# The last 64 rows of w1 by eight small transfers, a result sum in two PSUM tiles, and twice as many block-turned key groups in four batches

## Chip, core, metric

One core of a Trainium2 chip. The metric is the device time of one execution in microseconds, the median of several runs; comparisons are made with runs of the kernel before on the same chip.

## What is computed

One decode step of a gated mix: `g * a + (1 - g) * b` for 8 sequences of one token, 448 channels, in bf16.

```python
g = sigmoid((A_x * gate_w).sum(-1, keepdims=True))            # one gate per sequence
# a: attention over the last W = 1024 of 4096 cached positions, 16 query heads on 8 key heads, Dh = 256
q = (A_x @ A_wq).reshape(8, 1, 16, 256)
p = softmax(q . k[:, :, 3072:4096] * 256 ** -0.5)
a = (p . v[:, :, 3072:4096]).reshape(8, 1, 4096) @ A_wo       # 4096 x 448
# b: an MLP on the normalized A_x
y = layernorm(A_x)
b = gelu(y @ B_w1 + B_b1) @ B_w2 + B_b2                        # w1 448 x 1792, w2 1792 x 448
```

The keys and values that are read make 8 x 8 x 1024 x 256 x 2 tensors x 2 bytes, 67 MB of the 78 MB that the kernel reads.

## The kernel before

**The stream.** All large inputs go through a ring of four slots of 32 KB a partition (tile `slot`), in the order of a list: the keys of batch 0, wq, then keys of batch b and values of batch b - 1 in turn, then w1, the values of batch 7 with w2 behind them, and wo. A batch's keys or values are 4 MB, two transfers of 2 MB issued by SP (L128); weights are issued by SP at L140 and L157. `done()` frees a slot once its user's instructions are written down, and `pump()` then records the next load; on the chip SP waits at that load until the slot's readers have ended and until one of eight completion semaphores, used in turn by all loads, is free. SP works in order, so a load that waits holds up those behind it. x and the gate row are loaded by ACT, and so are the two biases (`biases`, L184), recorded in the transposing of batch 1's keys.

w1 has 448 rows. The first 384 lie on 128 partitions, three rows each (`w1_m`). The last 64 (`w1_t`) are cut in halves, so that one transfer of 128 rows of 896 elements fills all 128 partitions: even partitions hold a row's first half, odd ones its second. The same is done with the last 64 rows of wq.

**The batches.** For each batch b the kernel, in one fixed order per engine (nothing is reordered by a scheduler), does:

- `transpose_keys(b)`: sixteen groups of 4 x 128 columns (f32 words, two bf16 each) are turned so that the head dimension lies on the partitions. Group 0 is turned in 32 x 32 blocks by DVE into the tile `B` (`turn_blocks`, L330), and POOL puts the blocks in place in 16 copies (L338). Groups 1 to 15 go through PE (four transposes to a PSUM tile `ktp`, L360), and ten of them are copied to `kt` by ACT (L366), the other five by DVE (L368). Between the groups, at places given by `steps(b - 1)`, stand the softmax of the batch before (exponentials on ACT, `EB`, `EZ`, `ET` on DVE, one matmul `sm`) and the sums of the batch before that.
- `scores(b)`: 32 matmuls from `kt` (L427), which need all groups, POOL's too; `top(b)`, the row maximum on DVE (L440).
- `values(b - 1)`: 32 matmuls on the value slot into `PO` (L498).

**The MLP.** `norm` normalizes x, and `turned(1, ...)` lays it out as stationary operands `xw`; the shuffles of both biases follow in it (L307 to L310), recorded in the transposing of batch 2. `mlp_hidden` comes after the last batch's softmax: twelve matmuls for the first 384 rows (L538), and two for the last 64 (L549). Each of the two takes a stationary operand of 72 or 104 columns, zero in all but the wanted ones, so that one matmul serves two output blocks and even and odd partitions pick their halves.

**The end.** `hs` and the attention result `oP` are multiplied with w2 and wo: 40 wide matmuls into `A1` (L632), of 448 columns; `accs` is `A1` plus the bias (L639). The last six chunks of wo and the sum of `accs` over its four blocks go narrowly, 112 columns at a time, to four places of one PSUM tile, `A2` (L643). wo comes in seven pieces; the last four matmul chunks hang on the last two. `A2` is then copied to `res`, two blocks by DVE and two by ACT (L656), and each half is stored, by SP and by ACT (L657).

Of the kernel before, what the change touches and what calls it, by code (L numbers as in the profile page):

```python
# [11 lines left out]
BF16 = mybir.dt.bfloat16  # L12
F32 = mybir.dt.float32
# [4 lines left out]
def kernel(  # L18
# [15 lines left out]
    nc = tc.nc  # L34
# [19 lines left out]
    FQ = F // QD  # L54
    FB = FQ // BL
    HH = HD // 2
    FH = F // 2
    QN = 512
    NG = Hkv // QD
    SK = P // QD  # L60
    NCK = W // SK
    CB = 4
    UR = NG * rep
    HALF = D // 2
    DO = D // QD
# [79 lines left out]
    wq_m = A_wq[0:DM, :].rearrange("(p r) n -> p (r n)", r=NR)  # L145
    wq_t = A_wq[DM:D, :].rearrange("r (h n) -> (r h) n", h=2)
    w1_m = B_w1[0:DM, :].rearrange("(p r) f -> p (r f)", r=NR)
    w1_t = B_w1[DM:D, :].rearrange("r (h n) -> (r h) n", h=2)
    w2_v = B_w2.rearrange("(p c) n -> p (c n)", c=FB)
    wo_v = A_wo.rearrange("(q p j) n -> p q (j n)", p=P, j=J8)  # L150
    OW1T = NR * F
    OW2 = OW1T + FH
    wq_r = [wq_m[:, r * HD : (r + 1) * HD] for r in range(NR)]

    def last_values(t):
        kv_loader(A_v_cache, NB - 1, (2, 2), True)(t)
# [3 lines left out]
    add(("wq",), rows_loader(wq_r + [wq_t]))  # L160
    for b in range(1, NB):
        add(("k", b), kv_loader(A_k_cache, b))
        add(("v", b - 1), kv_loader(A_v_cache, b - 1))
    add(("w12",), rows_loader([w1_m, w1_t]))
    add(("v", NB - 1), last_values)
    cuts = [(q, 0, J8) for q in range(NQW - 2)] + [
        (NQW - 2, 0, 4),
# [14 lines left out]
    nc.scalar.dma_start(g_r[0:1, :], gate_w.rearrange("(o d) -> o d", o=1))  # L182

    def biases():  # L184
        nc.scalar.dma_start(b2_r[0:1, :], B_b2.rearrange("(o d) -> o d", o=1))
        nc.scalar.dma_start(b1_r[::BL, :], B_b1.rearrange("(t d) -> t d", t=QD))

    ident = consts.tile([P, P], BF16)
    make_identity(nc, ident[:])
# [23 lines left out]
    def turned(a, src):  # L213
        dst = xs[a][0:NB]
        nc.vector.tensor_copy(
            dst[:, 0:NR, :], src[:, 0:DM].rearrange("b (p r) -> b r p", r=NR)
        )
        for h in range(2):
            nc.vector.tensor_copy(dst[:, NR + h, h::2], src[:, DM:D])
        xt = work.tile([BL, NX, QD, BL], BF16, tag=f"w{2 + a}", name="xt")  # L220
        nc.vector.transpose(
            xt[:].rearrange("p r i b -> p (r i b)"),
            xs[a][:].rearrange("p r d -> p (r d)"),
        )
        for i in range(QD):
            nc.vector.tensor_copy(
                xw[BL * i : BL * (i + 1), a, :, BL : BL + NB], xt[:, :, i, 0:NB]
            )
# [66 lines left out]
    def norm():  # L295
        nc.vector.reciprocal(rstd[:], rstd[:])
        y_sb = consts.tile([NB, D], BF16)
        nc.vector.tensor_scalar(
            y_sb[:],
            x_sb[:],  # L300
            scalar1=mv[:, 0:1],
            scalar2=rstd[:],
            op0=ALU.subtract,
            op1=ALU.mult,
        )
        turned(1, y_sb[:])
        nc.vector.stream_shuffle(b1_b[:], b1_r[:], [0] * BL)  # L307
        b2_b = work.tile([BL, D], BF16, tag="w1", name="b2_b")
        nc.vector.stream_shuffle(b2_b[:], b2_r[:], [0] * BL)
        nc.vector.tensor_scalar_mul(b2s[0:NB, :], b2_b[0:NB, :], om[:])  # L310
# [4 lines left out]
        o = (a * NX + r) * GAP + BL  # L315
        return flat[:, o : o + NB]

    def ends(a, x2):
        o = (a * NX + NR) * GAP
        m = GAP + NB + BL * x2  # L320
        o += 0 if x2 else BL
        return flat[:, o : o + m], m
# [2 lines left out]

    BY_ACT = (1, 3, 4, 6, 7, 8, 10, 11, 13, 15)

    def turn_blocks(kn, kt, c0):
        B = epool.tile([P, CB, QD, SK // QD, QD], F32, tag="B", name="B")
        nc.vector.transpose(  # L330
            B[:].rearrange("p c w s a -> p (c w s a)"),
            kn[:, c0 * P : (c0 + CB) * P],
        )
        S8 = SK // QD
        words = kt[:].bitcast(F32)
        for w in range(QD):
            for g in range(QD):
                nc.gpsimd.tensor_copy(  # L338
                    words[BL * w : BL * (w + 1), :, c0 : c0 + CB, g * S8 : (g + 1) * S8, 0],
                    B[BL * g : BL * (g + 1), :, w].rearrange("p c s a -> p a c s"),  # L340
                )

    def transpose_keys(b, between=None):
        between = between or {}
        kn = slot("k", b)[:].bitcast(F32)
        for hh in range(NG):
            kt = ktpool.tile([P, QD, NCK, SK, NJ], BF16, tag="kt", name="kt")
            KT[hh] = kt
            for i in range(NCK // CB):
                g = hh * (NCK // CB) + i  # L350
                if g == 0:
                    turn_blocks(kn, kt, 0)
                    for step in between.get(g, ()):
                        step()
                    continue
                ktp = ps_kt.tile([P, CB, P, NJ], BF16, tag="ktp", name="ktp")
                words = ktp[:].bitcast(F32)
                for c in range(CB):
                    o = (hh * NCK + i * CB + c) * P
                    nc.tensor.transpose(  # L360
                        words[:, c, :, 0], kn[:, o : o + P], ident_f[:]
                    )
                dst = kt[:, :, i * CB : (i + 1) * CB, :, :]
                src = ktp[:].rearrange("p c (s a) t -> p a c s t", a=QD)
                if g in BY_ACT:
                    nc.scalar.copy(dst, src)  # L366
                else:
                    nc.vector.tensor_copy(dst, src)  # L368
                for step in between.get(g, ()):
                    step()  # L370
        done()

    def query():
        w = slot("wq")
        for r in range(NR):
            for n in range(W // QN):
                for t in range(QD):
                    o = r * HD + t * W + n * QN
                    nc.tensor.matmul(
                        S_ps[BL * t : BL * t + NB, n * QN : (n + 1) * QN],  # L380
                        lhsT=stationary(0, r),
                        rhs=w[:, o : o + QN],
                        start=(r == 0),
                        stop=False,
                        skip_group_check=True,
                    )
        for n in range(W // QN):
            for x2 in range(2):
                lhsT, m = ends(0, x2)
# [12 lines left out]
        qt = work.tile([P, 2, rep, QD, NJ, BL], BF16, tag="w2", name="qt")  # L402
        for h in range(2):
            nc.vector.transpose(  # L404
                qt[:, h].rearrange("p r i j b -> p (r i) j b"),
                qs[:, h * W // 2 : (h + 1) * W // 2].rearrange(
                    "p (m e j) -> p m j e", e=BL, j=NJ
                ),
            )
        qv = qw[:].rearrange("p j b t (u m) -> p j b t u m", u=NG)  # L410
        for i in range(QD):
            for g in range(QD):
                dst = qv[
                    BL * i : BL * (i + 1), :, :, 2 * (g % 2) : 2 * (g % 2) + 2, g // 2, 0:rep
                ]
# [115 lines left out]
    def mlp_hidden():  # L531
# [3 lines left out]
        for r in range(NR):  # L535
            for t in range(QD):
# [6 lines left out]
                    stop=False,  # L543
                    skip_group_check=True,
                )
        for x2 in range(2):
            lhsT, m = ends(1, x2)
            o = OW1T + x2 * FQ
            nc.tensor.matmul(  # L549
                hp[0:m, :],  # L550
                lhsT=lhsT,
                rhs=w[:, o : o + FQ],
                start=False,
                stop=(x2 == 1),
                skip_group_check=True,
            )
        z = work.tile([P, FQ], F32, tag="w0", name="z")
# [22 lines left out]
    def steps(b):  # L580
# [12 lines left out]
            d[15] = [biases]  # L593
        if b == 1:
            d[14] = [norm]
        return d

    transpose_keys(0, {7: [moments]})
# [20 lines left out]
    finish(b)  # L619
    spread(b)  # L620

    A2 = ps_kt.tile([P, DO], F32, tag="ktp", name="A2")
    w2 = slot("w12")
    w = slot("wo")
    NCH = NQW * J8
# [15 lines left out]
    for i, (lhsT, rhs) in enumerate(narrow):  # L641
        for t in range(QD):
            nc.tensor.matmul(  # L643
                A2[BL * t : BL * t + NB, :],
                lhsT=lhsT,
                rhs=rhs[:, t * DO : (t + 1) * DO],
                start=(i == 0),
                stop=(i == TAIL),
            )
    for h, (eng, copy) in enumerate(  # L650
# [2 lines left out]
        res = consts.tile([NB, 2, DO], BF16, name=f"res{h}")  # L653
        for i in range(2):
            t = 2 * h + i
            copy(res[:, i, :], A2[BL * t : BL * t + NB, :])  # L656
        eng.dma_start(  # L657
            out_f[:, h * HALF : (h + 1) * HALF], res[:].rearrange("b i d -> b (i d)")
        )
# [30 lines left out]
```

## Time and profile before

| | us |
|---|---|
| runs, median (three: 193.46 to 194.31) | 194.25 |
| profiled execution, its own time | 193.19 |
| its span, from first to last instruction | 191.4 |
| DMA queue q1, busy share of 16 engines | 96.3% |
| PE / DVE / ACT / POOL busy | 119.1 / 108.7 / 91.9 / 55.4 |
| mean rate of the DMA engines | 407 GB/s |
| granted clock of TensorE, mean | 0.854 |

The page describes the profiled execution. Its slices cut the span into 40 equal parts of 4.8 us; a digit is a busy share in tenths. "Idle before" of a group is the time its engine stood before it, with what ended it. Issue-to-landing times of DMAs include their wait in the queue. The trace also has a record for every DMA packet: queue, size, start and duration. q8 and q14 fetch instructions, q1 carries SP's transfers and q10 ACT's. All times in the text count from the first instruction, unless said otherwise.

### The profile page before, as it was taken

The page shows a single profiled execution, that of the slowest core. Times are in us where ns is not written, and L with a number is a line of the kernel's source. Part 1 is how long each engine was busy: PE and PEld are TensorE (multiplying, and loading weights), DVE is VectorE, ACT ScalarE, POOL GpSimd, SP SyncE. Part 2 cuts the span into 40 slices and gives each one's busy share as a digit, 9 for nine tenths or more (in the row PEclk, how much of TensorE's full clock was granted, in tenths as well). Part 3 has the DMA queues.
Part 4 walks back from the last instruction along what each step waited for, and adds up shares of the span by engine and source line. Part 5 has one row for each costly group of instructions (what it writes and reads, how often), then busy time and mean ns, then how long its engine had stood idle before and what let it go on. Part 6 is the DMA issues. An engine that isn't in the chain of part 4 may idle for free.

```text
span 191.4 us, 2916 instructions
## 1 busy us (share of the span) xinstructions
PE 119.1 (62%) x1114; PEld 77.0 (40%) x1114; DVE 108.7 (57%) x248; ACT 91.9 (48%) x105; POOL 55.4 (29%) x143
## 2 busy tenths in 40 slices
PE   0658509679784397738773676669854885083552
PEld 0646104555671185317641563168514761010111
DVE  4284673964889467705870687037822885847311
ACT  2298420894992259525852594228822892000001
POOL 8480000570750066005700480049002910000000
PEclk9999855999999969996999999756997999855555
DMA  5999999999999999999999999999999999999980
GB/s 204 445 402 425 440 435 419 425 421 432 422 430 428 428 421 431 426 431 428 418 431 425 421 435 428 428 428 416 431 431 428 425 425 420 403 422 430 407 321 3
DMA packets 7129, 77.86 MB, mean 407 GB/s; under 512 B 830, under 2 KB 1228, under 8 KB 1996
## 3 DMA queue, kind: packets, MB, share of 16 engines
q1 hardware_dynamic: 7072, 77.67, 96.3%
q8 instruction: 8, 0.13, 0.3%
q14 instruction: 5, 0.04, 0.1%
q10 hardware_dynamic: 44, 0.02, 0.0%
HBM read 77.67 MB, written 0.01 MB: 406 GB/s over the span
## 4 chain that ended last, share of the span: by engine, by line
DMA 73%; PE 10%; DVE 7%; ACT 4%; SPq 2%; issue 2%; DVEq 0%; ACTq 0%
DMA slot<-in_A_k_cache_dram 42%; DMA slot<-in_A_v_cache_dram 14%; DMA slot<-in_A_wq_dram 9%; DMA slot<-in_A_wo_dram 8%; PE ktp L360 7%; ACT kt L366 3%; DVE kt L368 2%; PE S_ps L427 2%; DVE qw L419 1%; SPq L128 1%; SPq L140 1%; DVE EZ L462 1%; PE S_ps L391 1%; DVE qt L404 1%; DVE nmx L440 1%
## 5 line engine op out<-in xcount | busy, mean ns | idle before, releaser
L366 ACT COPY kt<-ktp 128x1024 bf16<-128x1024 bf16 x80 | 76.1, 1024 | 37.0 <-PE ktp L360 36.9
L360 PE MATMUL ktp<-ident_f,slot 128*128 128x128 f32 x480 | 71.7, 305 | 31.4 <-DMA slot<-in_A_k_cache_dram 22.9
L360 PEld LDWEIGHTS ktp<-ident_f,slot 128*128 128x128 f32 x480 | 60.2, 157 | 49.2 <-issue 23.6
L338 POOL COPY kt<-B 32x128 f32<-32x128 f32 x128 | 51.3, 401 | 97.8 <-DVE B L330 86.3
L368 DVE COPY kt<-ktp 128x1024 bf16<-128x1024 bf16 x40 | 27.5, 689 | 16.9 <-PE ktp L360 16.5
L498 PE MATMUL PO<-slot,ET 128*16 128x512 bf16 x256 | 18.1, 429 | 16.2 <-DMA slot<-in_A_v_cache_dram 16.2
L444 ACT ACTIVATE E<-S_ps,nmx 128x1024 f32<-128x1024 f32 x8 | 8.9, 1114 | 28.7 <-DVE nmx L440 28.7
L330 DVE STREAM_TRANSPOSE B<-slot 128x512 f32<-128x512 f32 x8 | 5.7, 711 | 29.7 <-DMA slot<-in_A_k_cache_dram 29.6
L427 PE MATMUL S_ps<-kt,qw 128*4 128x512 bf16 x256 | 17.9, 419 | 5.4 <-DVE qw L419 5.4
L498 PEld LDWEIGHTS <-ET 128*16 128x16 bf16 x256 | 6.1, 94 | 27.6 <-DMA slot<-in_A_v_cache_dram 21.0
L440 DVE TENSOR_REDUCE nmx<-S_ps 128x1 f32<-128x1024 f32 x8 | 9.8, 1222 | 10.0 <-PE S_ps L427 10.0
L427 PEld LDWEIGHTS <-qw 128*4 128x4 bf16 x256 | 6.6, 85 | 14.0 <-DVE qw L419 6.5
L451 DVE STREAM_TRANSPOSE EB<-E 128x1056 f32<-128x1056 f32 x8 | 10.2, 1271 | 1.3 <-ACT E L444 1.3
L524 DVE TENSOR_TENSOR oP<-Y 32x32 bf16<-32x32 f32 x32 | 9.4, 295 | 1.1
L656 ACT CAST res<-A 8x112 bf16<-8x112 f32 x2 | 0.5, 246 | 15.8 <-DVE res L656 15.8
L481 DVE TENSOR_TENSOR ET<-sm,mask 128x512 bf16<-128x512 f32 x8 | 5.5, 692 | 2.2 <-PE sm L473 2.1
L511 DVE STREAM_TRANSPOSE T<-PO 128x512 f32<-128x512 f32 x8 | 5.7, 709 | 1.0 <-PE PO L498 0.9
L566 ACT ACTIVATE zb<-za 128x448 f32<-128x448 f32 x1 | 0.6, 577 | 10.8 <-DVE za L565 10.8
L473 PE MATMUL sm<-EZ,perm 128*128 128x128 bf16 x8 | 1.7, 216 | 6.0 <-DVE EZ L462 5.9
L632 PE MATMUL A<-slot,oP 128*8 128x448 bf16 x26 | 3.5, 547 | 2.5 <-DMA slot<-in_A_wo_dram 2.5
L639 DVE TENSOR_TENSOR accs<-A,b2s 128x448 f32<-128x448 f32 x1 | 0.6, 624 | 7.1 <-PE A L632 7.1
L516 DVE TENSOR_TENSOR Y<-T 64x64 f32<-64x64 f32 x16 | 4.0, 248 | 0.5
(91 smaller groups left out, 58.1 us busy)
## 6 DMA issues: line engine op xcount, KB each, us to landing
slot<-in_A_k_cache_dram SPq DMA_DIRECT2D x15, 2048.0 KB, 28.1
slot<-in_A_v_cache_dram SPq DMA_DIRECT2D x14, 2048.0 KB, 30.2
slot<-in_A_v_cache_dram SPq DMA_DIRECT2D x4, 1024.0 KB, 23.9
slot<-in_A_wq_dram SPq DMA_DIRECT2D x3, 1024.0 KB, 17.1
slot<-in_A_k_cache_dram SPq DMA_DIRECT2D x2, 1024.0 KB, 6.4
slot<-in_A_wo_dram SPq DMA_DIRECT2D x2, 896.0 KB, 18.7
slot<-in_B_w_dram SPq DMA_DIRECT2D x1, 1568.0 KB
slot<-in_B_w_dram SPq DMA_DIRECT2D x1, 1344.0 KB, 26.4
```

What stands on the lines that cost most here:

```text
L330: nc.vector.transpose(B[:].rearrange("p c w s a -> p (c w s a)"), kn[:, c0 * P : (c0 + CB) * P],)
L338: nc.gpsimd.tensor_copy(words[BL * w : BL * (w + 1), :, c0 : c0 + CB, g * S8 : (g + 1) * S8, 0], B[BL * g : BL * (g + 1), :, w].rearrange( ...
L360: nc.tensor.transpose(words[:, c, :, 0], kn[:, o : o + P], ident_f[:])
L366: nc.scalar.copy(dst, src)
L368: nc.vector.tensor_copy(dst, src)
L427: nc.tensor.matmul(S_ps[BL * t : BL * t + UR, n * QN : (n + 1) * QN], lhsT=qw[:, j, b, t, rep * u : rep * u + UR], rhs=KT[u][:, t, n * CQ ...
L440: nc.vector.reduce_max(nmx[:], S_ps[:], axis=AXIS.X, negate=True)
L444: nc.scalar.activation(E[:, 0:W], S_ps[:], ACT.Exp, bias=soft.pop(b)[:], scale=1.0, accum_out=E[:, W : W + 1],)
L451: nc.vector.transpose(EB[:].rearrange("p c r -> p (c r)"), E[:])
L498: nc.tensor.matmul(PO[BL * t : BL * t + Hq], lhsT=ET[:, c].rearrange("p u a r -> p (u a r)"), rhs=vn[:, c], start=(c < QD), stop=(c >= NCK ...
L511: nc.vector.transpose(T[:], PO[:].rearrange("p u (e j) -> p u j e", j=J8))
L524: nc.vector.tensor_tensor(oP[BL * i : BL * (i + 1), :, :, b], Yv[0:BL, :, :, i], Yv[BL : 2 * BL, :, :, i], op=ALU.add,)
```

## The change

Three things, and what follows from them.

1. The last 64 rows of w1 no longer go in halves over 128 partitions. They lie whole on partitions 0 to 63 of a tile of their own, `w1x`, and are loaded by eight transfers of 8 rows: transfer r takes rows r, r + 8, ..., r + 56 to the partitions of the same numbers. One stands behind each batch's value load in the stream's order, the eighth behind w1. `mlp_hidden` then takes four matmuls over 64 partitions, one for each output block, in place of the two wide ones. `turned(1, ...)` makes one copy fewer.
2. `A2` becomes two PSUM tiles, one for each half of the result: DVE's two copies read the first, ACT's the second.
3. In batches 2 to 5 (`DOUBLE`) the first two groups are turned by DVE and POOL, in one block transpose of twice the width and 16 copies of twice the size; PE and ACT turn one group fewer there.

The two bias loads move from ACT's queue to SP's, and the shuffles that use them from batch 2's transposing to batch 4's.

```diff
-    FH = F // 2
+    DOUBLE = (2, 3, 4, 5)
...
-    w1_t = B_w1[DM:D, :].rearrange("r (h n) -> (r h) n", h=2)
+    w1_t = B_w1[DM:D, :].rearrange("(i r) n -> r i n", r=DT // NB)
+    w1x = consts.tile([DT, F], BF16)
...
+    def with_rows(load, r):
+        def both(t):
+            load(t)
+            nc.sync.dma_start(w1x[r :: DT // NB, :], w1_t[r])
+
+        return both
...
-        add(("v", b - 1), kv_loader(A_v_cache, b - 1))
-    add(("w12",), rows_loader([w1_m, w1_t]))
+        add(("v", b - 1), with_rows(kv_loader(A_v_cache, b - 1), b - 1))
+    add(("w12",), with_rows(rows_loader([w1_m]), NB - 1))
...
     def biases():
-        nc.scalar.dma_start(b2_r[0:1, :], B_b2.rearrange("(o d) -> o d", o=1))
-        nc.scalar.dma_start(b1_r[::BL, :], B_b1.rearrange("(t d) -> t d", t=QD))
+        nc.sync.dma_start(b2_r[0:1, :], B_b2.rearrange("(o d) -> o d", o=1))
+        nc.sync.dma_start(b1_r[::BL, :], B_b1.rearrange("(t d) -> t d", t=QD))
...
-    def turn_blocks(kn, kt, c0):
-        B = epool.tile([P, CB, QD, SK // QD, QD], F32, tag="B", name="B")
+    def turn_blocks(kn, kt, n):
+        B = epool.tile([P, n, QD, SK // QD, QD], F32, tag="B", name="B")
...
-                if g == 0:
-                    turn_blocks(kn, kt, 0)
+                n = 2 if b in DOUBLE else 1
+                if g < n:
+                    if g == 0:
+                        turn_blocks(kn, kt, n * CB)
...
-        for x2 in range(2):
-            lhsT, m = ends(1, x2)
-            o = OW1T + x2 * FQ
+        for t in range(QD):
             nc.tensor.matmul(
-                hp[0:m, :],
-                lhsT=lhsT,
-                rhs=w[:, o : o + FQ],
+                hp[BL * t : BL * t + NB, :],
+                lhsT=stationary(1, NR)[0:DT, :],
+                rhs=w1x[:, t * FQ : (t + 1) * FQ],
                 start=False,
-                stop=(x2 == 1),
+                stop=True,
...
+        if b == 3:
+            d[14] = [spread_biases]
...
-    A2 = ps_kt.tile([P, DO], F32, tag="ktp", name="A2")
+    A2 = [ps_kt.tile([P, DO], F32, tag="ktp", name="A2") for h in range(2)]
...
-                A2[BL * t : BL * t + NB, :],
+                A2[t // 2][BL * t : BL * t + NB, :],
...
-            copy(res[:, i, :], A2[BL * t : BL * t + NB, :])
+            copy(res[:, i, :], A2[h][BL * t : BL * t + NB, :])
```

More of the change, by code (lines that the diff above doesn't have):

```diff
@@ L147 @@
     w1_m = B_w1[0:DM, :].rearrange("(p r) f -> p (r f)", r=NR)
-    w1_t = B_w1[DM:D, :].rearrange("r (h n) -> (r h) n", h=2)
+    w1_t = B_w1[DM:D, :].rearrange("(i r) n -> r i n", r=DT // NB)
+    w1x = consts.tile([DT, F], BF16)
     w2_v = B_w2.rearrange("(p c) n -> p (c n)", c=FB)
     wo_v = A_wo.rearrange("(q p j) n -> p q (j n)", p=P, j=J8)
-    OW1T = NR * F
-    OW2 = OW1T + FH
+    OW2 = NR * F
     wq_r = [wq_m[:, r * HD : (r + 1) * HD] for r in range(NR)]
+    def with_rows(load, r):
[3 more added lines that the diff above has]
+        return both
     def last_values(t):
@@ L217, in turned @@
         )
-        for h in range(2):
-            nc.vector.tensor_copy(dst[:, NR + h, h::2], src[:, DM:D])
+        if a:
+            nc.vector.tensor_copy(dst[:, NR, 0:DT], src[:, DM:D])
+        else:
+            for h in range(2):
+                nc.vector.tensor_copy(dst[:, NR + h, h::2], src[:, DM:D])
         xt = work.tile([BL, NX, QD, BL], BF16, tag=f"w{2 + a}", name="xt")
@@ L306, in norm, with spread_biases @@
         turned(1, y_sb[:])
+    def spread_biases():
         nc.vector.stream_shuffle(b1_b[:], b1_r[:], [0] * BL)
@@ L316, in stationary, with ends @@
         return flat[:, o : o + NB]
-    def ends(a, x2):
-        o = (a * NX + NR) * GAP
+    def ends(x2):
+        o = NR * GAP
         m = GAP + NB + BL * x2
@@ L326 @@
     BY_ACT = (1, 3, 4, 6, 7, 8, 10, 11, 13, 15)
-    def turn_blocks(kn, kt, c0):
-        B = epool.tile([P, CB, QD, SK // QD, QD], F32, tag="B", name="B")
+    def turn_blocks(kn, kt, n):
+        B = epool.tile([P, n, QD, SK // QD, QD], F32, tag="B", name="B")
         nc.vector.transpose(
             B[:].rearrange("p c w s a -> p (c w s a)"),
-            kn[:, c0 * P : (c0 + CB) * P],
+            kn[:, 0 : n * P],
         )
@@ L338, in turn_blocks @@
                 nc.gpsimd.tensor_copy(
-                    words[BL * w : BL * (w + 1), :, c0 : c0 + CB, g * S8 : (g + 1) * S8, 0],
+                    words[BL * w : BL * (w + 1), :, 0:n, g * S8 : (g + 1) * S8, 0],
                     B[BL * g : BL * (g + 1), :, w].rearrange("p c s a -> p a c s"),
@@ L388, in query @@
             for x2 in range(2):
-                lhsT, m = ends(0, x2)
+                lhsT, m = ends(x2)
                 o = NR * HD + x2 * W + n * QN
```

## The prediction

> **What bounds the kernel now.** I read the page's slices and its queue table first, then the stretches around the end, then the timeline of the last microseconds with the waits, then the tile `B`. The DMA rows of the page:
>
> ```profile
> DMA  5999999999999999999999999999999999999980
> ...
> q1 hardware_dynamic: 7072, 77.67, 96.3%
> q8 instruction: 8, 0.13, 0.3%
> q14 instruction: 5, 0.04, 0.1%
> ...
> slot<-in_A_k_cache_dram SPq DMA_DIRECT2D x15, 2048.0 KB, 28.1
> ```
>
> All sixteen DMA engines are busy from the first slice to the last but two: the kernel is one unbroken stream of 77.67 MB, and the compute engines (62% at most) run in its shadow. A 2 MB load lands 28.1 us after its issue, though its packets pass in about 4.9 us, so the queue always holds work ahead. The chain of waits begins its last link at the output weights' DMA. The end of the stream, by stretches (us; busy us and counts of PE, PEld, DVE, ACT, POOL; clock, DMA share, GB/s):
>
> ```profile
> 184.00:185.00 1.00, 0.41 (x8) 0.09 (x4) 0.00 (x0) 0.00 (x0) 0.00 (x0) 0.50 0.95 358
> 185.00:185.50 0.50, 0.47 (x6) 0.09 (x2) 0.00 (x0) 0.00 (x0) 0.00 (x0) 0.50 0.72 283
> 185.50:186.00 0.50, 0.44 (x2) 0.00 (x0) 0.02 (x1) 0.00 (x0) 0.00 (x0) 0.50 0.55 212
> 186.00:186.50 0.50, 0.00 (x0) 0.00 (x0) 0.50 (x1) 0.00 (x0) 0.00 (x0) 0.50 0.32 118
> ```
>
> The share decays over 1.5 us: the engines do not finish together. The trace's packet records tell who is late. Packets of one engine follow each other within a few ns, so those of q1 sort into 16 chains. Their ends, from the span's start: seven at 184.60 to 185.46, eight at 186.18 to 186.42, one at 186.56. The eight each carry one of the eight 16 KB q8 fetches, a hole of about 1.05 us and a slowed packet beside it. The last carries two of the 8 KB q14 fetches, about 0.96 us each. Every transfer needs all of its engines, so the last one dates them all. After it:
>
> ```profile
> 185.98 0.62 DVE L639 TENSOR_TENSOR accs<-A,b2s 128x448 f32<-128x448 f32 x1 [7.10 <-PE A L632]
> 186.51 0.54 PE L643 MATMUL A<-slot,oP 128*8 128x112 bf16 x16 [0.56 <-DMA slot<-in_A_wo_dram]
> ...
> 187.21 0.40 PE L643 MATMUL A<-slot,oP 128*8 128x112 bf16 x8
> 187.64 0.56 DVE L656 CAST res<-A 8x112 bf16<-8x112 f32 x2 [1.03 <-PE A L643]
> 188.23 0.36 SPq L657 DMA_DIRECT2D out_dram<-res  x1
> 188.29 0.50 ACT L656 CAST res<-A 8x112 bf16<-8x112 f32 x2 [15.77 <-DVE res L656]
> 188.82 0.31 ACTq L657 DMA_DIRECT2D out_dram<-res  x1
> ```
>
> ACT's two copies begin only when DVE's two end, though both read finished sums: 0.6 us in which the second half of the result waits for the first.
>
> **Part by part. Two PSUM tiles for A2.** With a tile of its own ACT waits for PE alone. It would start about 0.05 us after PE's end at 187.61 instead of at 188.29, take the same 0.50, and issue its store at about 188.20, beside SP's at 188.23. Stores land 1.23 us after issue (188.23 to 189.46, 188.82 to 190.05), so the later one lands at 189.46 rather than 190.05: 0.59 us less. The bounds are 0.59 and nothing (the two stores colliding, or the wait staying). I take 0.57, near the full value, because no other wait stands before ACT.
>
> **The last 64 rows of w1.** Before: one transfer of 128 rows of 1792 B, on all 16 engines, eight packets each at a spacing of 71 ns plus 6 for the semaphore's packet, 0.57 us per engine. After: eight transfers of 8 rows of 3584 B; the bytes are the same. An 8-row transfer is spread over 8 engines, as the store of the first result half shows (window 188.9 to 189.3: 8 data and 8 semaphore packets):
>
> ```profile
> DMA packets 16, 0.00 MB, mean 9 GB/s; under 512 B 16, under 2 KB 16, under 8 KB 16
> ...
> q1 hardware_dynamic: 16, 0.00, 5.1%
> ```
>
> The 3584 B packets of the output weights stand 141 ns apart, so each w1 transfer costs 0.141 + 0.006 on its engine, eight cost 1.18. Eight engines gain 1.18 - 0.57 = 0.61 us of work, the other eight lose 0.57. Which eight decides the sign. No 8-row transfer runs inside the stream, but the 4-row one of b1 does: its packets sit in four chains, three of the seven early ones and the last one. If eight rows use those four and four more, the last engine goes to 186.56 + 0.61 = 187.17, while the eight with q8 fetches, if they are the others, drop to 185.61 to 185.85. Beside these rows: by the Trainium skill, "DMA: Bandwidth & Descriptors", section "Why a DMA increments its semaphore by 16 and not by 1", a transfer takes the largest count up to 16 that divides its outer dimension, and the lowest-numbered engines. The trace agrees on the count (8 and 8); engine numbers are not in the records. All the weights' landings move by +0.61, and PE, DVE and the stores behind them. The bounds: -0.57 if the late engine is not among the eight, +0.61 if it is, more if small transfers cost beyond their bytes (a rival). I take +0.61, on the 4-row transfer's row.
>
> **Two block-turned groups in batches 2 to 5.** Per batch, off PE four transposes (0.66 us), off ACT one copy (1.02), onto DVE a transpose of 1024 columns for one of 512 (711 ns; the 1056-column one of L451 takes 1271, so +0.53), onto POOL 16 copies of twice the size:
>
> ```profile
> L338 POOL COPY kt<-B x128: 384/400/442, 7.0 to 153.5; 32x128 f32<-32x128 f32 x128
> ```
>
> At best they stay 0.40, at worst I allow twice, 0.80, with 0.042 between them; I take the worst: 16 x 0.84 = 13.5 us. In batch 5, keys landed at 106.53, POOL ended at 114.53 and the last `kt` copy at 117.50. POOL would now end at 106.62 + 1.24 + 0.15 + 13.5 = 121.5, and `scores` begins 4 us later. Queued behind it on PE are `values` of the batch before and the next transposes; SP waits for `values` to free a slot. Scores (2.0) and the row maximum (1.24) end near 124.8, before the next keys at 126.06. And the stream does not feel it: the shortest wait from issue to landing of a full key load was 23.1 us (44.20 to 67.32), less 4.9 of its own, so some 18 us of work lie ahead of any late issue. Cost: nothing.
>
> **At nothing, too.** The two bias loads leave ACT's queue for SP's, behind a value load; they wait for two earlier landings there, and SP's next key load, which waits for slot and keys until 44.2 anyway, is behind them. Their users now run in batch 4's transposing, two batches later, still some 60 us before `hp` is read. The eight issues cost SP about 0.6 us each, and each takes one of the eight completion semaphores that SP's loads reuse in turn, so a load may wait for the eighth before it: at least five of those eight are 2 MB, 24 us of work. Four 64-row matmuls for two wide ones (0.96 us) on `hp` end before PE's wait of 3.09 us for values at 174.41.
>
> **Sum.** 193.19 (its span 191.4 and 1.8 around it) + 0.61 - 0.57 = 193.23. The median of the runs stands 1.06 above the profiled execution; carried over, 194.25 + 0.04 = 194.3.
>
> **Rivals.** *The stream ends earlier.* If the engine that is last in the profiled execution is not last in ordinary ones, or not among the eight, the end falls to the next: 186.42 now, and after the change 185.46 + 0.61 = 186.07, the latest of the early seven. That is 0.35 to 0.5 off the stream, with the tail's 0.57 about -0.95: 193.3. For it: only 0.14 us separates the last engine from the eight. Against: its two fetches and its place in the 4-row transfer. Even a perfect balance (the 16 ends' mean is 185.7) gives 0.85 + 0.57 and no more: 192.8.
>
> *Small transfers cost more than their bytes: slower.* The nearest row is b1's: its data packet ended 0.61 us before its semaphore packet, on an engine busy with 16 KB packets of the other queue. Were each of the eight transfers to hold up its ring like this, 8 x 0.61 = 4.9 us are added, 199.2; it decides from 0.12 us per transfer (0.97 in all). Against it: inside q1 the semaphore packet and the next transfer follow within 6 ns. The Trainium skill, same page, section "Rules for kernel authors", speaks for it: under 64 KB a transfer pays mostly overhead, and these have 28 KB. No run here yet shows such a transfer inside the stream.
>
> *POOL becomes the bound: slower.* If a copy of 256 strided elements takes over 1.1 us, a batch's chain (1.4 + 16 x 1.14 + 3.2) passes the 19.5 us between key loads; at 1.5 us, four batches run over by 9 each and eat the 18 us, +15 or so. Nothing in 384 to 442 ns points there.
>
> *The split does not free ACT* (the wait stays for another reason): +0.61 alone, 194.9.
>
> **How the numbers follow.** As summed, 0.42, its own range 193.9 to 194.8. Earlier stream, 0.27. Costly small transfers, 0.20, mostly between 195.4 and 197. POOL, 0.04. ACT not freed, 0.07. About 0.5%, 0.97 us, is what a measurement of this kernel can tell from no change. Faster by more: 0.20, most of the second case. Slower by more: 0.26, the third, the POOL case and a little of the last. The rest, 0.54, within. The range 193.0 to 195.9 leaves out the dear half of the small transfers, POOL and the best of the balance.
>
> **What would show it.** Right: the DMA share decays over more than 1.5 us before the end; the last weights' piece lands some 0.6 us later; ACT's and DVE's copies of `res` start together and the stores go out together; the eight loads of `w1x` leave the stream at 9s. POOL's copies near 0.8 us and `scores` waiting for them. Wrong: ACT's copies still behind DVE's; the last piece landing earlier, or over a microsecond later; a slice of DMA under 9 in mid-stream.

## Result: 0.43% slower

| | before | after |
|---|---|---|
| median, us (14 runs each, same chip) | 193.40 (193.00 to 194.31) | 194.41 (194.21 to 194.69) |
| ratio, 95% interval | | 1.0043 [1.0028, 1.0058] |
| profiled execution, us / its span | 193.19 / 191.4 | 194.35 / 192.5 |
| last piece of wo landed | 186.46 | 188.38 |
| from there to the end of the span | 4.9 | 4.2 |

The change costs 0.83 us [0.54, 1.12], the ratio and this figure being those of the means (193.61 and 194.45 us); the medians are 1.01 apart. That is within the 0.5% that the prediction called no difference, though the interval excludes zero and reaches a little past it. The forecast of 194.3 stands 0.1 us beside the 194.41, but not because its sum was right. The median of before over 14 runs is 193.40, not the 194.25 of three, and the median of after stands 1.01 above it, not 0.04: two misses of 0.85 and 0.97 us that cancel. That the forecast lies so near is luck.

The page of after, the DMA rows. The stream is whole, as before:

```profile
DMA  5999999999999999999999999999999999999970
...
q1 hardware_dynamic: 7066, 77.67, 96.2%
```

The end of the stream of after, by stretches (columns as in the prediction; the last two are DMA share and GB/s):

```profile
184.00:185.00 1.00, 0.47 (x8) 0.23 (x8) 0.00 (x0) 0.00 (x0) 0.00 (x0) 0.50 1.02 393
...
186.00:186.50 0.50, 0.20 (x4) 0.00 (x0) 0.00 (x0) 0.00 (x0) 0.00 (x0) 0.50 0.80 305
186.50:187.00 0.50, 0.23 (x4) 0.09 (x4) 0.00 (x0) 0.00 (x0) 0.00 (x0) 0.50 0.37 140
187.00:187.50 0.50, 0.48 (x6) 0.09 (x2) 0.00 (x0) 0.00 (x0) 0.00 (x0) 0.50 0.20 79
187.50:188.00 0.50, 0.37 (x2) 0.00 (x0) 0.09 (x1) 0.00 (x0) 0.00 (x0) 0.50 0.11 43
```

At 186.0 to 186.5 the share is still 0.80, where it was 0.32 before: about thirteen engines are still at work, so more are late than the eight that carry w1. The thin end is longer too: from 187.0 to 188.0, two or three engines of sixteen work alone, then one. The last microseconds of after, from the timeline (start, duration, engine, instruction, idle before and what ended it):

```profile
187.91 0.62 DVE L653 TENSOR_TENSOR accs<-A,b2s 128x448 f32<-128x448 f32 x1 [6.70 <-PE A L646]
188.42 0.55 PE L657 MATMUL A<-slot,oP 128*8 128x112 bf16 x16 [0.55 <-DMA slot<-in_A_wo_dram]
...
189.12 0.40 PE L657 MATMUL A<-slot,oP 128*8 128x112 bf16 x8
189.56 0.54 DVE L670 CAST res<-A 8x112 bf16<-8x112 f32 x2 [1.02 <-PE A L657]
189.60 0.50 ACT L670 CAST res<-A 8x112 bf16<-8x112 f32 x2 [13.71 <-PE A L657]
190.13 0.32 SPq L671 DMA_DIRECT2D out_dram<-res  x1
190.13 0.30 ACTq L671 DMA_DIRECT2D out_dram<-res  x1
```

The weights' last wait ends 1.9 us later than before (188.42 for 186.51). Behind it the split does what was forecast: ACT's copies wait for PE, not for DVE, and both stores go out at 190.13.

Middle of the stream, windows of 20 us, after:

```profile
60.00:80.00 20.00, 13.05 (x121) 7.91 (x121) 16.02 (x31) 9.74 (x11) 10.19 (x17) 0.91 1.01 423
80.00:100.00 20.00, 13.19 (x125) 9.46 (x128) 12.84 (x22) 9.68 (x11) 10.04 (x16) 0.91 1.00 423
100.00:120.00 20.00, 13.25 (x133) 9.13 (x129) 15.27 (x28) 9.98 (x12) 10.01 (x16) 0.91 1.01 424
120.00:140.00 20.00, 14.56 (x153) 9.53 (x145) 10.98 (x22) 10.86 (x12) 6.35 (x16) 0.91 1.01 424
```

The same of e2_old_rows below, which differs from after only in how the last rows of w1 are loaded and used:

```profile
60.00:80.00 20.00, 13.13 (x129) 9.41 (x125) 15.80 (x32) 9.83 (x11) 9.99 (x16) 0.91 1.01 428
80.00:100.00 20.00, 13.18 (x136) 8.93 (x129) 13.91 (x25) 9.83 (x11) 10.04 (x16) 0.91 1.01 427
100.00:120.00 20.00, 11.83 (x129) 7.62 (x125) 14.09 (x27) 9.74 (x11) 10.02 (x16) 0.98 1.00 426
120.00:140.00 20.00, 14.07 (x145) 8.57 (x137) 11.95 (x22) 11.23 (x13) 6.43 (x16) 0.94 1.01 428
```

The DMA share is full in both, so the slices cannot show a loss. The rate can: 423 to 424 GB/s for 426 to 428, although after moves the w1 bytes in these windows besides. Engines that are "busy" move less. The packet records say how: of the 3712 packets of 16 KB, 15 took over 640 ns before, 183 do after (the usual time is about 610), and they lie where the w1 transfers pass: some 16 to 43 at each of the six that run amid 16 KB packets. (The seventh and eighth run beside the first 384 rows of w1, in packets of 10752 B: 34 of these take over 420 ns, none before.) They lie on engines that carry no w1 row too. Summed over the stream from 30 us on, the packets of q1 take 0.86 us an engine longer than before, 0.73 of it in the 16 KB ones; in e2_old_rows the same sum is within 0.01 of before's. A batch's 32 packets took 19.58 us on every engine before; after, 19.69 to 19.71 on the engines without w1 (+0.11 per transfer), 19.83 to 19.88 on those with it (its own 0.147 more).

### The profile page after: what moved, and what is told of

Same layout as the page of the kernel before. It is cut to its first block, busy times and chain, and to the rows that moved or that the text cites. A ratio compares the mean times of both kernels' runs of the same rounds, so it can differ in the third digit from the quotient of the medians.

```text
span 192.5 us, 2886 instructions
## 1 busy us (share of the span) xinstructions
PE 118.8 (62%) x1100; PEld 73.8 (38%) x1100; DVE 118.6 (62%) x247; ACT 88.2 (46%) x101; POOL 69.7 (36%) x143
## 4 chain that ended last, share of the span: by engine, by line
DMA 83%; POOL 5%; PE 5%; DVE 3%; ACT 2%; issue 1%; DVEq 0%; POOLq 0%
DMA slot<-in_A_k_cache_dram 46%; DMA slot<-in_A_v_cache_dram 29%; DMA slot<-in_A_wo_dram 8%; POOL kt L350 5%; PE ktp L374 3%; PE S_ps L441 2%; ACT kt L380 1%; DVE B L342 1%; PE A L657 1%; DVE xt L231 0%; DVE xw L236 0%; DVE stats L256 0%; DVE xs L222 0%; DVE xs L229 0%; ACT rstd L258 0%
## 5 line engine op out<-in xcount | busy, mean ns | idle before, releaser
L350 POOL COPY kt<-B 32x128 f32<-32x128 f32 (+1 forms) x128 | 65.5, 512 | 85.4 <-DVE B L342 80.4
L380 ACT COPY kt<-ktp 128x1024 bf16<-128x1024 bf16 x76 | 72.4, 1021 | 37.3 <-PE ktp L374 37.2
L374 PE MATMUL ktp<-ident_f,slot 128*128 128x128 f32 x464 | 68.4, 299 | 31.3 <-DMA slot<-in_A_k_cache_dram 22.4
L374 PEld LDWEIGHTS ktp<-ident_f,slot 128*128 128x128 f32 x464 | 55.9, 153 | 52.6 <-issue 29.0
L382 DVE COPY kt<-ktp 128x1024 bf16<-128x1024 bf16 x40 | 27.3, 683 | 11.9 <-PE ktp L374 11.7
L512 PE MATMUL PO<-slot,ET 128*16 128x512 bf16 x256 | 20.4, 471 | 10.1 <-DMA slot<-in_A_v_cache_dram 10.1
L441 PE MATMUL S_ps<-kt,qw 128*4 128x512 bf16 x256 | 19.3, 445 | 11.3 <-POOL kt L350 5.9
L342 DVE STREAM_TRANSPOSE B<-slot 128x512 f32<-128x512 f32 (+1 forms) x8 | 7.8, 978 | 26.7 <-DMA slot<-in_A_k_cache_dram 26.7
L512 PEld LDWEIGHTS <-ET 128*16 128x16 bf16 x256 | 6.9, 102 | 22.6 <-DMA slot<-in_A_v_cache_dram 12.7
L538 DVE TENSOR_TENSOR oP<-Y 32x32 bf16<-32x32 f32 x32 | 13.7, 429 | 1.1
L530 DVE TENSOR_TENSOR Y<-T 64x64 f32<-64x64 f32 x16 | 7.2, 451 | 0.6
```

Of the source, the lines that this page charges most:

```text
L342: nc.vector.transpose(B[:].rearrange("p c w s a -> p (c w s a)"), kn[:, 0 : n * P],)
L350: nc.gpsimd.tensor_copy(words[BL * w : BL * (w + 1), :, 0:n, g * S8 : (g + 1) * S8, 0], B[BL * g : BL * (g + 1), :, w].rearrange("p c s a ...
L374: nc.tensor.transpose(words[:, c, :, 0], kn[:, o : o + P], ident_f[:])
L441: nc.tensor.matmul(S_ps[BL * t : BL * t + UR, n * QN : (n + 1) * QN], lhsT=qw[:, j, b, t, rep * u : rep * u + UR], rhs=KT[u][:, t, n * CQ ...
L512: nc.tensor.matmul(PO[BL * t : BL * t + Hq], lhsT=ET[:, c].rearrange("p u a r -> p (u a r)"), rhs=vn[:, c], start=(c < QD), stop=(c >= NCK ...
L530: nc.vector.tensor_tensor(Y[:, :, u, :], T[0 : 2 * BL, u, :, k], T[2 * BL : P, u, :, k], op=ALU.add)
```

## Experiments

Ratios are to the kernel before, run on the same chip. The questions: what each part is worth, and why packets that are not w1's get slower. Each expectation names its theories and their rivals.

**e1: the two PSUM tiles alone.**

```diff
 (before)
-    A2 = ps_kt.tile([P, DO], F32, tag="ktp", name="A2")
+    A2 = [ps_kt.tile([P, DO], F32, tag="ktp", name="A2") for h in range(2)]
...
```

> The kernel before with A2 in two PSUM tiles and nothing else. All theories of the stream expect the same here: the stream is untouched, ACT's copies of res start with DVE's, 0.6 to 0.8 us off the end (the changed kernel's tail, from the last piece's landing to the end of the span, was 0.78 us shorter than before's). Ratio 0.996 to 0.997. Rival: the stores collide and the gain is under 0.3 us.

Measured: 192.94 us, 0.9969 [0.9952, 0.9987], that is -0.6 us [-0.93, -0.25]. Its timeline has the pair of copies and the pair of stores:

```profile
187.76 0.54 DVE L656 CAST res<-A 8x112 bf16<-8x112 f32 x2 [1.04 <-PE A L643]
187.80 0.50 ACT L656 CAST res<-A 8x112 bf16<-8x112 f32 x2 [13.85 <-PE A L643]
188.33 0.36 SPq L657 DMA_DIRECT2D out_dram<-res  x1
188.34 0.32 ACTq L657 DMA_DIRECT2D out_dram<-res  x1
```

From the landing of the last piece of wo to the end of the span are 4.6 us in this trace (186.58 to 191.2), 0.3 less than before. So the expected 0.6 to 0.8 us is not in the trace: the 0.78 that it was taken from, after's shorter end, has a second part, which e11 shows.

**e2: after, with the last rows of w1 as before; e5: the new rows alone.**

```diff
 (e2, from after)
-    w1_t = B_w1[DM:D, :].rearrange("(i r) n -> r i n", r=DT // NB)
+    w1_t = B_w1[DM:D, :].rearrange("r (h n) -> (r h) n", h=2)
...
-        add(("v", b - 1), with_rows(kv_loader(A_v_cache, b - 1), b - 1))
-    add(("w12",), with_rows(rows_loader([w1_m]), NB - 1))
+        add(("v", b - 1), kv_loader(A_v_cache, b - 1))
+    add(("w12",), rows_loader([w1_m, w1_t]))
...
```

e5 makes the opposite edit to before.

> The changed kernel with the last 64 rows of w1 loaded and used as before (one transfer of 128 half rows, two wide matmuls); two tiles, doubled groups and bias loads on SP stay. If the eight row transfers carry the whole loss: as the kernel with two tiles alone, ratio 0.996 to 0.997, last engine near 186.6, no packets of 16 KB over 650 ns but those beside instruction fetches. Rival, that doubled groups or the bias loads disturb the stream: ratio at or above 1.000 and slow packets still there.

> The kernel before with the eight 8-row transfers of w1's last rows and their four matmuls, and nothing else: one store still waits for the other, the bias loads stay on ACT. If the parts add up: the difference between the changed kernel and the one with the old rows (1.0043 against 0.9941, some 2.0 us) on top of before, ratio 1.008 to 1.011. Rival, that the doubled groups or the tiles are needed for the loss: under 1.005.

Measured: e2 192.43, 0.9941 [0.9917, 0.9964]; e5 195.02, 1.0086 [1.0055, 1.0117]. By the two ratios, 1.0043 against 0.9941, the rows cost 2.0 us (+-0.5) in after; e5 alone gives 1.7 [1.1, 2.3]. The prediction had 0.61, below both. e2 has the lowest median of all kernels here and beats both: 1.0% under after, 0.6% under before.

**e8: the doubled groups alone.**

```diff
 (before)
+    DOUBLE = (2, 3, 4, 5)
...
+                n = 2 if b in DOUBLE else 1
+                if g < n:
+                    if g == 0:
+                        turn_blocks(kn, kt, n * CB)
...
```

> The kernel before with two block-turned groups in batches 2 to 5 and nothing else. If the stream does not feel the compute engines: ratio 0.998 to 1.002, POOL's copies of 256 elements near 0.66 us in pitch, scores waiting for POOL in four batches. Rival, that the later scores delay a load: ratio above 1.003 and slices of DMA under 9 in mid-stream.

Measured: 193.26, 0.9989 [0.9975, 1.0002]: nothing, as the prediction had it. `scores` waits 7.0 us in all for POOL, under the stream.

**e11: two tiles and the later biases.** e1, with the bias loads on SP and their shuffles in batch 4's transposing; only the doubled groups are then missing from e2.

```diff
 (e1)
-        nc.scalar.dma_start(b2_r[0:1, :], B_b2.rearrange("(o d) -> o d", o=1))
+        nc.sync.dma_start(b2_r[0:1, :], B_b2.rearrange("(o d) -> o d", o=1))
...
+    def spread_biases():
...
+        if b == 3:
+            d[14] = [spread_biases]
```

> The kernel before with the two tiles and the two bias loads on SP, old rows and one block-turned group in every batch. SP's program has a hole of 0.45 us ahead of its 80th instruction in every trace so far; in the kernel before and with two tiles alone it lies behind the stores' landing, in e2_old_rows ahead of it. If that is why e2_old_rows is 0.5 us faster than two tiles alone: as e2_old_rows, ratio 0.994 to 0.995, and the doubled groups are worth nothing. Rival, that the doubled groups bring it: ratio 0.997.

Measured: 192.66, 0.9962 [0.9945, 0.9979], not told apart from e2 or from e1 by the intervals. The traces do show a difference to e1: from the later store's issue to the end of the span, 2.9 us in e1 (188.34 to 191.2), 2.4 in e11 (188.20 to 190.6). In e1, as in before, SP stands idle for 0.44 us behind the stores' landing, ahead of the 80th instruction that the records have of it. Nine of the fourteen traces show such a hole of 0.44 to 0.46 us at the 80th instruction; in the other five a wait ends there or shortly before. In e11, with two more instructions on SP (the bias loads), the 80th lies within the wait for the landing, and no hole follows it. The traces of all kernels that issue both stores together fall into two groups: where the hole lies behind the landing (e1, e3, e12, e13, e14) the end is 2.85 to 3.1 us behind the later store's issue, elsewhere (after, e2, e4, e6, e9, e11) 2.3 to 2.5. So the bias move gained 0.4 to 0.5 us at the end of the profiled executions (lowest times: 192.75 in e1, 192.34 in e11); the medians of separate sets do not resolve it.

**e3: four transfers of 16 rows.** Sixteen rows fill all sixteen engines evenly; if only the uneven load cost time, it goes.

```diff
 (after)
-    w1_t = B_w1[DM:D, :].rearrange("(i r) n -> r i n", r=DT // NB)
+    w1_t = B_w1[DM:D, :].rearrange("(i r) n -> r i n", r=4)
...
-            nc.sync.dma_start(w1x[r :: DT // NB, :], w1_t[r])
+            if r % 2:
+                nc.sync.dma_start(w1x[r // 2 :: 4, :], w1_t[r // 2])
```

> The changed kernel with four transfers of 16 rows instead of eight of 8 rows; same bytes, rows still far apart in memory, but all 16 engines take one packet each. Theory out-of-step (a transfer on eight engines shifts them against the other eight, and all sixteen lose some 0.11 us until they run evenly again): no slow packets around these transfers, even load, last engine at 186.6, ratio 0.996 to 0.997. Rival far-rows (reading eight rows 28 KB apart is what slows everyone): slow packets stay, four times 0.11 = 0.4 us, ratio about 0.999. Rival small-transfer (each small transfer costs, whatever its shape): also 0.4 us, ratio about 0.999.

Measured: 193.75, 1.0004 [0.9988, 1.0021]. Better than after by 0.4%, still 1.2 us over e2. Where a transfer passes there are 23, 38 and 38 slow 16 KB packets (at about 60, 100 and 140 us), at the places between none: 0.15 to 0.2 us per engine and transfer. Uneven load is part of the loss, not the slow packets' cause. The 1.2 us over e2 are explained: the packets of q1 take 0.80 us an engine longer than before, nearly as in after, and SP's hole of 0.46 us lies in the tail here.

**e4: eight neighbouring rows for each transfer, to neighbouring partitions.**

```diff
 (after)
-    w1_t = B_w1[DM:D, :].rearrange("(i r) n -> r i n", r=DT // NB)
+    w1_t = B_w1[DM:D, :].rearrange("(r i) n -> r i n", r=DT // NB)
...
-            nc.sync.dma_start(w1x[r :: DT // NB, :], w1_t[r])
+            nc.sync.dma_start(w1x[r * NB : (r + 1) * NB, :], w1_t[r])
```

> The changed kernel with its eight 8-row transfers, but each takes eight rows that follow each other in memory, to eight partitions that follow each other. Theory out-of-step: nothing changes, ratio 1.003 to 1.006, packets of 650 to 700 ns around each transfer on all engines. Rival far-rows: the slow packets go, 0.85 us less, ratio 0.999 to 1.001. Rival small-transfer: nothing changes.

Measured: 194.75, 1.0059 [1.0042, 1.0075]; 140 slow packets. The stride of the rows is not the cause.

**e9: e2 and eight dummy transfers of 8 rows, from values that were read just before, to an unused tile.** It adds 0.23 MB and leaves w1 as it was.

```diff
 (e2)
+    hot = consts.tile([DT, F], BF16)
...
+            v = A_v_cache[r, 0, kv_base : kv_base + NB * NCK, :].rearrange(
+                "(i c) d -> i (c d)", c=NCK
+            )
+            nc.sync.dma_start(hot[r :: DT // NB, :], v[:, 0:F])
...
```

> The kernel with the old rows of w1 (e2_old_rows), plus eight 8-row transfers of 3584 B rows at the places where the changed kernel has its own, which read values that the transfer just before them has read, into a tile that nobody uses. The bytes put 1.18 us more on eight engines. Theory small-transfer: slow packets on all engines as in the changed kernel, 0.85 us more, 2.0 us over e2_old_rows, ratio 1.004 to 1.006. Rival cold-source: no slow packets, 1.2 us over e2_old_rows, ratio 1.000 to 1.001.

Measured: 194.87, 1.0067 [1.0043, 1.0091]: 2.4 us over e2, of which the bytes explain at most 8 x 0.147 = 1.2 on an engine. 226 slow packets. Which memory is read, and whether it was read before, is not the cause.

**e13: e2 and four dummy transfers of 16 rows to every eighth of the 128 partitions** (one run, no interval).

```diff
 (e2)
+    hot = consts.tile([P, F], BF16)
...
+            if r % 2:
+                v = A_v_cache[r, 0, kv_base : kv_base + 2 * NB * NCK, :].rearrange(
+                    "(i c) d -> i (c d)", c=NCK
+                )
+                nc.sync.dma_start(hot[r :: NB, :], v[:, 0:F])
...
```

> e2_old_rows plus four transfers of 16 rows of 3584 B that read values just read and go to every eighth of 128 partitions of a tile nobody uses, behind the values of batches 1, 3 and 5 and behind w1. [...] If the small transfer as such stretches the packets in flight: slow packets near 60, 100 and 140 us, 0.15 to 0.2 us an engine each time, as with sixteen rows on 64 partitions. [...] The bytes alone add 0.6 us.

Measured: 194.98 in its run. At its places some 55 to 63 slow packets, about 0.3 us per engine each: spreading the destination does not help. Which engine filled which partitions the records do not say, so the run does not settle whether engines get in each other's way at the partitions that they write.

**e6: all eight transfers together behind w1.**

```diff
 (after)
-            nc.sync.dma_start(w1x[r :: DT // NB, :], w1_t[r])
+            for i in range(NB):
+                nc.sync.dma_start(w1x[i :: DT // NB, :], w1_t[i])
...
-        add(("v", b - 1), with_rows(kv_loader(A_v_cache, b - 1), b - 1))
+        add(("v", b - 1), kv_loader(A_v_cache, b - 1))
```

> The changed kernel with its eight 8-row transfers all behind the first 384 rows of w1, at the end of the stream, instead of one behind each batch's values. Theory small-transfer (each one stretches all packets in flight by some 0.11 us): the loss stays, ratio 1.003 to 1.005. Rival cold-source (a read of w1 amid keys and values is what stalls all engines, since nothing near it was read lately; here w1's other rows have just been read): the slow packets go, only the uneven load of 0.6 us is left, ratio 0.998 to 1.000.

Measured: 196.16, 1.0128 [1.0102, 1.0155], and mostly for a reason of its own, so the time says nothing on the question. SP's rows of its timeline (the stretch of eight issues takes 27.3 us, the waits between them included):

```profile
138.00 27.30 SPq L159 DMA_DIRECT2D w1x<-in_B_w_dram  x8
165.40 2.59 SPq L128 DMA_DIRECT2D slot<-in_A_v_cache_dram  x4
```

Eight small loads take all eight completion semaphores in turn. Each is issued only when the load that held its semaphore before has landed, the last at 164.74, when w1's first 384 rows have; SP, which works in order, comes to the next load at 165.40. By then no work lies ahead: the DMA rate falls to 0 at 165 to 166. The prediction named this limit and found at least five large loads among any eight; in after there are four in one place (around the bias loads) and five or more elsewhere, in this kernel none. The small loads pass here beside w1's first 384 rows, which were being read: 24 of their packets of 10752 B take over 420 ns, none in before. So a transfer that follows other rows of w1 slows its neighbours too, which agrees with e9.

**e12: e2 with the old transfer of 128 half rows in mid-stream, behind batch 4's values** (one run). **e14: all 64 whole rows in one transfer at the same place.** Both move 224 KB over all sixteen engines; e12 in 128 pieces of 1792 B to 128 partitions, e14 in 64 of 3584 B to 64.

```diff
 (e12, from e2)
+    w1h = consts.tile([P, FH], BF16)
...
+            nc.sync.dma_start(w1h[:], w1_t)
 (e14, from after)
-    w1_t = B_w1[DM:D, :].rearrange("(i r) n -> r i n", r=DT // NB)
+    w1_t = B_w1[DM:D, :]
...
-            nc.sync.dma_start(w1x[r :: DT // NB, :], w1_t[r])
+            if r == NB // 2:
+                nc.sync.dma_start(w1x[:], w1_t)
```

> The kernel with the old rows (e2_old_rows), but their one transfer, 128 half rows of 1792 B, stands in mid-stream, behind the values of batch 4 (near 120 us), instead of behind w1. If any small transfer amid 16 KB packets stretches those in flight: packets of 650 ns and more on all engines near 120 to 122 us, some 0.1 us an engine. Rival few-rows (only transfers with one packet an engine do it): none there, as in e2_old_rows. The time says nothing at this size.

> The changed kernel with the 64 rows in one transfer, whole on 64 partitions as in the change, behind the values of batch 4: four rows of 3584 B for each of 16 engines. If the loss of the change comes from transfers of one packet an engine and from eight engines carrying all of them: no more than a tenth of the slow packets of the changed kernel, even load, ratio 0.994 to 0.996, as with the old rows. Rival, that 3584 B packets or the rows' places on 64 partitions are the cause: slow packets near 120 us on all engines, ratio near 0.996 to 0.998, since there is one such place only.

Measured: e12 192.97 in its run; e14 194.99, 1.0074 [1.0048, 1.0099]. Windows of 1 us at the place (the last two columns are DMA share and GB/s), e12:

```profile
119.00:120.00 1.00, 1.00 (x20) 0.38 (x22) 0.94 (x3) 0.00 (x0) 0.00 (x0) 1.00 0.98 397
120.00:121.00 1.00, 0.91 (x16) 0.18 (x8) 0.12 (x2) 0.00 (x0) 0.00 (x0) 1.00 1.03 427
121.00:122.00 1.00, 0.50 (x12) 0.27 (x16) 1.00 (x1) 0.00 (x0) 0.00 (x0) 1.00 1.04 434
```

and e14:

```profile
118.00:119.00 1.00, 0.16 (x4) 0.10 (x7) 0.93 (x3) 0.59 (x1) 0.74 (x2) 1.00 0.85 360
119.00:120.00 1.00, 1.00 (x24) 0.37 (x16) 0.96 (x2) 0.00 (x0) 0.00 (x0) 1.00 1.58 379
120.00:121.00 1.00, 0.83 (x16) 0.19 (x8) 0.12 (x1) 0.00 (x0) 0.00 (x0) 1.00 0.54 154
121.00:122.00 1.00, 0.00 (x0) 0.00 (x0) 1.00 (x1) 0.00 (x0) 0.00 (x0) 1.00 1.32 363
122.00:123.00 1.00, 0.40 (x8) 0.21 (x12) 0.10 (x1) 0.80 (x1) 0.00 (x0) 1.00 0.97 251
123.00:124.00 1.00, 1.00 (x24) 0.50 (x20) 0.00 (x0) 0.40 (x2) 0.00 (x0) 1.00 0.75 311
```

The share of a window counts a packet where it starts, so a share of 1.58 followed by 0.54 means packets longer than the window: 16 KB packets of up to 1576 ns. From 118 to 124 us e14 moves 1818 KB, at 427 GB/s it would be 2562: 744 KB, or 1.7 us of stream, are lost. e12 has twelve packets over 640 ns there and moves 426 GB/s, no loss that shows. So one transfer of 64 whole rows does as much harm as eight of 8, and the number of transfers is not what is paid for. That is against the theory put down for e14; its rival (3584 B packets or 64 partitions) is right that slow packets appear, but put the price far too low, at 0.996 to 0.998 for the measured 1.0074. (SP's hole lies in its tail too, 0.46 us.)

**What stays open.** Shown: loads of 8, 16 or 64 whole rows of 3584 B, amid loads of 16 KB packets, slow the packets of all sixteen engines; 128 half rows of the same bytes do not. Not the cause: uneven load (e3), the rows' stride (e4), the memory read (e9), the number of transfers (e14). e13 speaks against the destination's spread. Left are the number of partitions filled and the packet's size, which e14 changes together. The kernel before has a row that speaks against the size alone: the last load of wq, 128 half rows of 4096 B to 128 partitions, runs at 19.7 to 21.9 us beside 28 packets of 16 KB, and none of these takes more than 628 ns. wo's 3584 B packets on 128 partitions stand 141 ns apart with nothing slowed, but they have no 16 KB packets beside them. Against few partitions alone speak the bias loads, five packets of 896 B to a partition each, beside which 49 packets of 16 KB in before take at most 621 ns; these move only 4.5 KB, too little to settle it. So what is left is a row of some KB in a load that does not fill all partitions, whether by their number or by which engine writes which of them. No run separated these, and the cause stays open.

## Why the prediction was right and wrong

- **The bound: right.** In every kernel here the end follows the last piece of wo, and POOL's 14 us of added work (69.7 busy for 55.4) do not show.
- **Two tiles, -0.57: right in mechanism, the size between 0.3 and 0.6.** ACT waits for PE alone, and e1's runs give -0.6, with an interval that is wide; its trace gives 0.3. There, as in after, 0.2 goes to the two stores meeting: one lands 1.44 us after its issue in after, for 1.23 before. That was the bound "the two stores colliding", in part.
- **The w1 rows, +0.61: mis-sized; about 2.0.** This is the step that failed. The direction held: the late engine is among the eight, and it still ends last, at 188.48. But each transfer also costs the engines some 0.11 us in their other packets, and the packets of q1 take 0.86 us an engine longer in all. With the engine's own 0.61 that is 1.47 of the +1.92 in the profiled execution. The remaining 0.4 is not explained: the packets do not name their engine, so how late this one was at the start cannot be read with certainty, and the stream as a whole was not late there (the 256th packet of 16 KB has ended at 26.3 us, 26.5 before). The rival *small transfers cost more than their bytes* named the effect and its threshold, 0.12 us per transfer; the runs lie about on it. It looked for the price in the transfer's own ring, at b1's 0.61; it was paid by the neighbours' packets, at 0.11. The Trainium skill, "DMA: Bandwidth & Descriptors", "Rules for kernel authors", puts full bandwidth at 128 partitions and at least 1 MiB a transfer and calls those under 64 KB mostly overhead. The sign agrees for the 28 KB transfers; e14's 224 KB in one transfer to 64 partitions are the dearest per place, 1.7 us, while e12's 224 KB to 128 partitions are free, so the runs agree with the first part of the rule, the 128 partitions, and not with the least size.
- **"The eight with q8 fetches, if they are the others": wrong for two.** Two engines with a 16 KB instruction fetch also seem to carry w1 rows (as far as their packets can be sorted by engine); they end at 187.62 and 187.92, next to last. This did not move the end.
- **Doubled groups, nothing: right, on terms too dear.** The tile `B` of after, the wide copies in batch 5, and the wait of `scores`:

```profile
L350 POOL COPY kt<-B x128: 384/516/707, 6.5 to 155.4; 32x128 f32<-32x128 f32 x64, 32x256 f32<-32x256 f32 x64
```

```profile
108.81 10.63 POOL L350 COPY kt<-B 32x256 f32<-32x256 f32 x16 [9.03 <-DVE B L342]
119.50 2.00 PE L441 MATMUL S_ps<-kt,qw 128*4 128x512 bf16 x32 [1.37 <-POOL kt L350]
```

  Sixteen copies take 10.63 us, 0.66 each for the 0.84 allowed; `scores` waits 1.4 us and begins at 119.5, where 121.5 was reckoned. (The 4 us later of the prediction count from the last copy at 117.50; before's `scores` began at 116.35, ahead of it.) The stream feels none of it.
- **Biases "at nothing": a missed gain.** The loads cost nothing, but with two more instructions on SP its 0.45 us hole no longer stands in the tail. A step can be worth something although nobody waits for it, if it shifts what an engine executes last.
- **The sum.** By measured parts: -0.6 (tiles), about -0.45 (SP's hole; from the traces), 0 (groups), +2.0 (rows) = +0.95, against +0.83 measured. By the two profiled executions alone: +1.92 (landing of the last weights), -0.78 (what follows it: 0.3 the tiles, 0.45 SP's hole) = +1.14, against 1.16 between their times. The forecast had -0.57, 0, 0, +0.61. It stayed within 0.5% because the gain that it missed offsets a third of the cost that it missed.
- **The median carried over was wrong**: 1.06 over the profiled execution from three runs, 0.21 from fourteen. Before's runs spread over 193.0 to 194.3, so three do not fix its level.
- **"A slice of DMA under 9" as the sign of a costly transfer: useless.** The engines stay busy while they slow down; only the rate and the packet times show it. The other sign, the last piece over a microsecond later, came true.

## What to carry over

In a stream that fills the DMA engines, cost a new transfer by what it does to its neighbours' packets, and read the rate, not the busy share: the same 224 KB went free as 128 rows on 128 partitions and cost 1.7 us as 64 rows. Keep the odd remainder in a shape that fills all partitions, even at the price of an extra matmul operand: of the shapes tried for these 224 KB, no other was free. And when parts of a change have opposite signs, measure them apart: after without its w1 part is 192.43, which neither kernel reaches.

## Of the hardware, not expected

- A 16 KB packet takes about 610 ns, and 640 to about 930, a few in e4 to 1067, beside a transfer of 8 or 16 rows of 3584 B (e14: up to 1576), also on engines that carry none of that transfer.
- SP stands for 0.44 to 0.46 us ahead of its 80th recorded instruction in nine of fourteen traces; in the others a wait ends there or before and hides it, if it is there. Its cause was not tried; whether it costs time depends on what SP then has to do.
- Engines do not finish evenly: in before, sorted as in the prediction, the seven with no instruction fetch end 0.7 to 2 us ahead of the nine with one or two, so there the end of the stream is dated by where fetches fall.
- DVE's additions into `oP` (32 of 32x32) take 429 ns on average in after, 295 before. The doubled groups do it: 446 in e8, which has only them, 294 in e1 and e11, which lack them. They run beside POOL's copies, which take longer there; that this is the reason was not tried. DVE is not what the end waits for, so it costs nothing here.
